# Three fused layers on one core: the scaling of the attention's exponentials on ScalarE, and v's rows laid out as long runs

## The chip, the cores and the metric

The kernel runs on one core of a Trainium2 chip. The metric is the device time of one execution in microseconds (us); lower is better. The engines are TensorE (PE), VectorE (DVE), ScalarE (ACT), GpSimd (POOL) and SyncE (SP), which issues the transfers here. Each works through its own list of instructions in order.

## What is computed

Local attention with block summaries, then a dense two-layer block, then a mixture of 8 experts with a capacity:

```python
scores_l = scale * np.matmul(q, k.transpose(0, 1, 3, 2))      # (2, 8, 768, 768), kept where |i - j| < 16
scores_s = scale * np.einsum('bhsd,bhnd->bhsn', q, k_sum) + np.log(block)   # 24 block summaries
a = np.exp(scores_all - np.max(scores_all, axis=-1, keepdims=True))
a = a / (np.sum(a, axis=-1, keepdims=True) + 1e-09)
x = np.matmul(a, np.concatenate([v, v_sum], axis=2))
h = x @ w_in
g = np.where(h > 0.0, h, np.exp(np.minimum(h, 0.0)) - 1.0)
x = g @ w_out                                                  # 1536 tokens, 512 -> 2048 -> 512
# then: every token goes to its best of 8 experts (relu MLP 512 -> 1024 -> 512), scaled by its gate
```

All of it is in float32. Matmuls of the dense layers split each operand into a high and a low part and add three products.

## The kernel before

Attention runs on 16 items `p`, a pair of heads for half a batch entry each, and each item in two **slots** `u` (32 in all) of three query blocks of 64. A block of 64 queries sees 96 keys around it and 24 block summaries, 120 columns. In a slot (names of the code):

- `pe_s` (L225): PE computes the scores S for three blocks.
- `dve_max` (L236): DVE adds the mask and takes the extreme; `act_exp` (L249): ACT takes three exponentials of 128x120 with their sums.
- `norm` (L256): DVE adds 1e-9 to the sums (L258) and takes the reciprocal (L259); POOL multiplies all three blocks by it in one operation of 128x360 (L260).
- `pe_t`, `act_t` (L263, L269): one slot later PE transposes the result, and ACT copies it from PSUM as pT (L271), at the start of the slot after that.
- `pe_o`, `act_o`, `dve_o`: PE multiplies pT by the tile `vw` (L279); ACT takes the high part of the result into xT (L288), DVE the low part (L293).

`vw` holds, for six query blocks, the 96 rows of v that each uses, and under them the 24 summaries. `load_vw` (L169) brings the 96 rows by one transfer on SP's queue from the padded v, whose rows are 512 values of all heads; 128 of them belong to a pair. `load_vs` (L217) brings the summaries from SBUF. `prep_k` and `prep_va` make the keys' windows and the summaries for the next item, in the first and the second slot of each item.

The dense layer starts in slot 8 while the attention still runs. `w_load`, `w_conv` and `w_split` bring a block of weights as float64 words, make float32 of them in three steps on DVE (L315, L319, L322), and split it: ACT casts the high part (L328), POOL subtracts it (L329). `mm1` (L340) is the first matmul into a PSUM tile h, of which there are two; `elu_exp` (two on ACT, L346 and L347), `elu_max` (DVE, L351), `g_hi` (ACT, L356) and `g_lo` (POOL, L360) make g; `mm2` (L373) is the second matmul.

The whole is written out in one order by hand (`manual_schedule`), in the loop over `sl` from L830 on. Slots 0 to 7 are attention and weight conversion (the head). Slots 9 to 16 are the `dense` ones, with a block of the first and of the second weights converted in most of them; the first matmul runs two blocks ahead in them, so that slots 15 and 16 have none. From slot 17 on the order is the same for each slot, with one weight block converted and put away in DRAM per slot. In the dense slots `norm` stands between the second and third step of the conversion.

Of the kernel before, what the change touches and what calls it, by code (L numbers as in the profile page):

```python
# [15 lines left out]
ALU = mybir.AluOpType  # L16
# [4 lines left out]
P = 128  # L21
NB, NH, S, D = 2, 8, 768, 64
NPAIR = NH // 2
WIN = 16
BLK = 32
NSUM = S // BLK
QB = 64
NQB = S // QB
WK = QB + 2 * WIN
KEYS = WK + NSUM  # L30
N = NB * S
DM = NH * D
# [5 lines left out]
TT = 384  # L38
NT = N // TT
BPT = TT // P  # L40
QPT = TT // QB
# [5 lines left out]
GRP = 3  # L47


def build(tc, cap, qT, kT, vT, vP, wi, wo, wg, wgT, wx, out):  # L50
    nc = tc.nc
    cap = max(0, min(int(cap), N))
    nj = -(-cap // P)
# [3 lines left out]
    with ctx:  # L57
# [26 lines left out]
        for hh in range(2):  # L84
# [3 lines left out]
                out=mv, in_=mv, pattern=[[0, 3], [1, WK]], compare_op=ALU.is_ge,  # L88
                fill=NEG, base=-1, channel_multiplier=-1)
            nc.gpsimd.affine_select(  # L90
                out=mv, in_=mv, pattern=[[0, 3], [-1, WK]], compare_op=ALU.is_ge,
# [8 lines left out]
            out=tri, in_=tri, pattern=[[1, P]], compare_op=ALU.is_gt,  # L100
# [68 lines left out]
        def load_vw(p):  # L169
            t, pr = divmod(p, NPAIR)  # L170
            b, half = divmod(t, 2)
            vw = apool.tile([P, QPT, P], F32, tag="vw", name=f"vw{p}")
            vbase = (b * (S + 2 * WIN) + half * TT) * DM + pr * P
            nc.sync.dma_start(
                vw[0:WK], bass.AP(vP.tensor, vbase, [[DM, WK], [QB * DM, QPT], [1, P]]))
            VW[p] = vw

        def prep_k(p):
# [18 lines left out]
        def prep_va(p):  # L197
            t, pr = divmod(p, NPAIR)
            if t % 2 == 0:
                nc.vector.tensor_reduce(  # L200
                    out=VA[p % 2][:, WK:KEYS], in_=VT[p].rearrange("p (u s) -> p u s", s=BLK),
                    op=ALU.add, axis=AX.X)
# [18 lines left out]
        def where(u):  # L221
            p, g = divmod(u, GPP)
            return p, p // NPAIR, p % NPAIR, g * GRP
# [32 lines left out]
        def norm(u):  # L256
            sc, st = SC[u], ST.pop(u)
            nc.vector.tensor_scalar(out=st[:, 2], in0=st[:, 1], scalar1=1e-9, scalar2=None, op0=ALU.add)  # L258
            nc.vector.reciprocal(out=st[:, 2], in_=st[:, 2])  # L259
            nc.gpsimd.tensor_tensor(  # L260
                sc, sc, st[:, 2].unsqueeze(2).to_broadcast([P, GRP, KEYS]), op=ALU.mult)

        def pe_t(u):  # L263
            pt = PT[u] = psm(f"T{u}", "T")
# [25 lines left out]
        def dve_o(u):  # L290
            p, t, pr, g0 = where(u)
            q = slice(g0 * QB, (g0 + GRP) * QB)
            nc.vector.tensor_tensor(  # L293
                xT[t][:, 1, pr, q], PS.pop(("o", u))[:, 0 : GRP * QB], xT[t][:, 0, pr, q].bitcast(F32),
                op=ALU.subtract)
# [10 lines left out]
        def w_conv(which, parts=(0, 1, 2)):  # L306
            for part in parts:
                for io, f in which:
                    if part == 0:
                        raw = RW[io, f]  # L310
                        t = mpool.tile([P, 512], U32, tag="t1", bufs=T1, name=f"t1{io}{f}")
                        RW[io, f] = (raw[:, :, 0], raw[:, :, 1], t)
                    lo, hi, t = RW[io, f]
                    if part == 0:
                        nc.vector.tensor_scalar(  # L315
                            out=t, in0=hi, scalar1=3, scalar2=0x3FFFFFF8,
                            op0=ALU.logical_shift_left, op1=ALU.bitwise_and)
                    elif part == 1:
                        nc.vector.scalar_tensor_tensor(  # L319
                            out=t, in0=hi, scalar=0xC0000000, in1=t, op0=ALU.bitwise_and, op1=ALU.bitwise_or)  # L320
                    else:
                        nc.vector.scalar_tensor_tensor(  # L322
                            out=t, in0=lo, scalar=29, in1=t, op0=ALU.logical_shift_right, op1=ALU.bitwise_or)
# [30 lines left out]
        def g_hi(t, f):  # L354
            gT[t, f] = mpool.tile([P, 2, TT], F32R, tag="g", name=f"g{t}_{f}")
            nc.scalar.copy(gT[t, f][:, 0], EP[t, f])  # L356

        def g_lo(t, f, eng):
            g = gT[t, f]
            eng.tensor_tensor(g[:, 1], EP.pop((t, f)), g[:, 0].bitcast(F32), op=ALU.subtract)  # L360
# [359 lines left out]
        st = {}  # L720
# [50 lines left out]
        load_k(1)  # L771
        load_q(1)
        load_vw(0)
        prep_k(0)
        prep_va(0)
        pe_va(0)
        load_vt(1)
        load_vw(1)


# [29 lines left out]
        def w_prefetch():  # L810
            if nload[0] >= len(order) or (order[nload[0]] in later and len(put) < len(later)):
                return
            io, f = order[nload[0]]
            nload[0] += 1
            if (io, f) in later:
                t = mpool.tile([P, 512], U32, tag="raw", bufs=4, name=f"rw{io}{f}")
                nc.sync.dma_start(t, wf[later.index((io, f))])
                RW[io, f] = (None, None, t)
            else:
                w_load(io, f)  # L820
# [9 lines left out]
        for sl in range(total):  # L830
            n = sl - LAG
            u, p = sl, sl // GPP
# [25 lines left out]
            def split_next():  # L858
                if wpend:
                    w_split(*wpend.pop(0))  # L860

            if sl == LAG - 1:
# [30 lines left out]
                act_exp(u)  # L893
                prep_k(p + 1)
                norm(u)
                g_hi(0, 0)
                g_lo(0, 0, nc.gpsimd)
# [22 lines left out]
            if u < NU and sl % GPP == 1 and p and p + 1 < NPR:  # L920
                load_vw(p + 1)
# [21 lines left out]
            if dense:  # L943
                if el:
                    g_hi(*el[1:])
                    g_lo(*el[1:], nc.gpsimd)
                split_next()
                split_next()
                if sl % GPP and p + 1 < NPR:
                    prep_va(p + 1)  # L950
                w_conv(cv, (0,))
                if u - 2 in late:
                    dve_o(u - 2)
                w_conv(cv, (1,))
                norm(u)
                w_conv(cv, (2,))
                for x in cv:
                    w_prefetch()
                wpend.extend(cv)
                cv = []  # L960
# [16 lines left out]
            if u < NU and not dense:  # L977
                norm(u)
# [80 lines left out]
            if gr == 1 and t == 0 and f == FPG:  # L1059
                pa.close()  # L1060
                qpool = ctx.enter_context(tc.tile_pool(name="qpool", bufs=2, side="right"))
                pr = ExitStack()
# [71 lines left out]
        for f in range(4, 8):  # L1134
# [4 lines left out]
            out=key, in0=sel0, scalar=float(32 * N * NE), in1=key, op0=ALU.mult, op1=ALU.add)  # L1139
# [3 lines left out]
            op=ALU.is_gt)  # L1143
# [6 lines left out]
            op=ALU.is_equal)  # L1150
# [27 lines left out]
        for v in range(3):  # L1178
            nc.vector.tensor_reduce(
                out=tabs[:, :, v].rearrange("p (k j) -> p k j", j=nj), in_=tmp[v], op=ALU.add, axis=AX.X)  # L1180
# [109 lines left out]
        large(1, cv1)  # L1290


_NAMES = ["qT", "kT", "vT", "vP", "wi", "wo", "wg", "wgT", "wx"]


def _layout(np, q, k, v, moe_w_in, moe_w_out, moe2_w_gate, moe2_w1, moe2_w2):
    c = np.ascontiguousarray
    qT = q.reshape(NB, NPAIR, 2, S, D).transpose(0, 1, 2, 4, 3).reshape(NB, NPAIR, P, S)
    kT = k.reshape(NB, NPAIR, 2, S, D).transpose(0, 1, 2, 4, 3).reshape(NB, NPAIR, P, S)
    kT = np.pad(kT, ((0, 0), (0, 0), (0, 0), (WIN, WIN)))  # L1300
    vT = v.reshape(NB, NPAIR, 2, S, D).transpose(0, 1, 2, 4, 3).reshape(NB, NPAIR, P, S)
    vP = np.pad(v.transpose(0, 2, 1, 3).reshape(NB, S, DM), ((0, 0), (WIN, WIN), (0, 0)))
    wi = moe_w_in.reshape(NCC, P, NFC, P).transpose(2, 1, 0, 3).reshape(NFC, P, 512)
    wo = moe_w_out.reshape(NFC, P, DM)
    wi, wo = c(wi).view(np.int64), c(wo).view(np.int64)
    wg = moe2_w_gate.reshape(NCC, P, NE).transpose(1, 0, 2)
    w1 = moe2_w1.reshape(NE, NCC, P, 2, 512).transpose(0, 2, 3, 1, 4).reshape(NE, P, 8, 512)
    w2 = moe2_w2.reshape(NE, 8, P, DM).transpose(0, 2, 1, 3)
    wx = np.concatenate([w1, w2], axis=2)
    return {"qT": c(qT), "kT": c(kT), "vT": c(vT), "vP": c(vP), "wi": c(wi), "wo": c(wo), "wg": c(wg), "wgT": c(moe2_w_gate.T), "wx": c(wx)}  # L1310


# [16 lines left out]
```

## Time and profile before

| | before |
|---|---|
| runs shown | 517.78, 516.6, 513.6 us (median 516.6) |
| the profiled execution | 517.51 us, of which the profile's span is 515.6 |
| PE busy | 481.3 us (93%) |
| DVE busy | 335.3 us (65%) |
| ACT busy | 270.3 us (52%) |
| POOL busy | 196.5 us (38%), of it the scaling L260 31.4 us in 32 operations |
| transfers | 79.98 MB, of it 16 loads vw of 288 KB |

Times within the profile count from the span's start. A row of the timeline gives the start of an instruction (or of several equal ones), how long it took from its start to its end, waiting for a resource included, its engine, line, operation, the tiles it writes and reads, and in brackets how long the engine stood idle before it and who released it.

### The profile page before, as it was taken

Reading aid. Unit: us, or ns where it says so; the run is one execution under the profiler, and the core shown is the slowest. Engines: PE = TensorE matmul, PEld = TensorE weight load, DVE = VectorE, ACT = ScalarE, POOL = GpSimd, SP = SyncE. Lnnn points to the kernel's source line nnn. Section 1 sums busy time; section 2 is a strip of 40 time slices with the busy share of each in tenths; the row PEclk is TensorE's granted clock in tenths of the full one; section 3 lists DMA queues with packets and bytes.
Section 4 is the critical chain, followed back from the end, with each engine's and each line's share of the span. In section 5 each row is a group of like instructions: output and inputs, shape, how many; then the busy total and the mean of one; then the engine's idle time right before and its main releaser. Section 6 shows DMA issues by size and latency. Waiting matters only on the chain. (4 is left out here: it accounts for less than half of the span.)

```text
span 515.6 us, 9263 instructions
## 1 busy us (share of the span) xinstructions
PE 481.3 (93%) x3052; PEld 414.0 (80%) x3052; DVE 335.3 (65%) x887; ACT 270.3 (52%) x688; POOL 196.5 (38%) x197
## 2 busy tenths in 40 slices
PE   6888798899999999999999999999998999999792
PEld 5576576688888888999999999888867989888682
DVE  3689999899888772111128979856686864556460
ACT  3846555675657546665333333333753865566350
POOL 4345575635333443785223323322335030040440
PEclk8988998999999999999999999999999999999897
DMA  8996555678776432438310010011644976357470
GB/s 219 258 266 200 168 177 188 207 231 257 210 192 185 160 103 66 112 112 285 123 52 11 0 62 0 2 62 57 211 142 144 334 220 225 124 182 252 147 244 15
DMA packets 45635, 79.98 MB, mean 155 GB/s; under 512 B 4604, under 2 KB 19196, under 8 KB 45552
## 3 DMA queue, kind: packets, MB, share of 16 engines
q1 hardware_dynamic: 43792, 73.83, 46.5%
q0 software_dynamic: 1760, 5.19, 3.3%
q8 instruction: 34, 0.56, 0.5%
q14 instruction: 49, 0.40, 0.3%
HBM read 65.29 MB, written 13.11 MB: 152 GB/s over the span
## 5 line engine op out<-in xcount | busy, mean ns | idle before, releaser
L340 PE MATMUL h<-xT,Wi 128*128 128x384 f32 x768 | 150.4, 344 | 8.3 <-DVE e L351 6.6
L340 PEld LDWEIGHTS h<-xT,Wi 128*128 128x128 f32 x768 | 138.2, 192 | 15.9 <-DVE e L351 8.8
L373 PE MATMUL acc<-Wo,g 128*128 128x512 f32 x576 | 146.8, 398 | 1.7 <-POOL Wo L329 1.0
L360 POOL TENSOR_TENSOR g<-e,g 128x384 fp32r<-128x384 f32 x63 | 77.2, 1226 | 124.2 <-ACT g L356 109.5
L373 PEld LDWEIGHTS acc<-Wo,g 128*128 128x128 f32 x576 | 105.3, 188 | 23.7 <-POOL g L360 1.4
L351 DVE SCALAR_TENSOR_TENSOR e<-e,h 128x384 f32<-128x384 f32 x64 | 35.3, 552 | 75.6 <-ACT e L347 75.6
L346 ACT ACTIVATE e<-h 128x384 f32<-128x384 f32 x64 | 31.6, 493 | 58.7 <-PE h L340 56.6
L260 POOL TENSOR_TENSOR sc<-sc,st 128x360 f32<-128x360 f32 x32 | 31.4, 980 | 68.6 <-DVE st L259 50.1
L565 DVE TENSOR_TENSOR E<-rawq,E 128x512 fp32r<-128x512 f32 x70 | 47.7, 722 | 10.9 <-ACT E L555 9.9
L252 ACT ACTIVATE sc<-sc,st 128x120 f32<-128x120 f32 x96 | 36.8, 385 | 28.7 <-DVE st L245 28.7
L356 ACT CAST g<-e 128x384 fp32r<-128x384 f32 x64 | 33.0, 516 | 33.0 <-DVE e L351 33.0
L697 PE MATMUL bh<-xbq,E 128*128 128x256 f32 (+1 forms) x288 | 43.6, 303 | 2.5 <-ACT ysf L601 1.4
L555 ACT CAST E<-rawq 128x512 fp32r<-128x512 f32 x75 | 42.5, 618 | 6.3 <-issue 3.2
L697 PEld LDWEIGHTS bh<-xbq,E 128*128 128x128 f32 x288 | 41.3, 188 | 4.8 <-ACT ysf L601 1.6
L686 PE MATMUL y<-E,g 128*128 128x512 f32 x168 | 41.7, 393 | 0.0
L435 DVE CUSTOM_DVE_ANT_0 dot<-a,wgb 128x512 f32<-128x512 f32 x48 | 40.0, 889 | 0.0
L686 PEld LDWEIGHTS y<-E,g 128*128 128x128 f32 x168 | 30.6, 188 | 5.7
L347 ACT ACTIVATE e<-e 128x384 f32<-128x384 f32 x64 | 33.7, 526 | 2.0
L271 ACT COPY pT<-T 120x384 f32<-120x384 f32 x32 | 15.3, 479 | 36.7 <-PE T L267 36.4
L245 DVE CUSTOM_DVE_ANT_0 sc<-S,masks 128x120 f32<-128x120 f32 x96 | 22.0, 277 | 11.1 <-PE S L231 10.3
L231 PE MATMUL S<-kw,qt 64*64 64x120 f32 x384 | 28.9, 287 | 0.0
L231 PEld LDWEIGHTS S<-kw,qt 64*64 64x64 f32 x384 | 21.3, 143 | 6.1 <-issue 3.9
(216 smaller groups left out, 621.5 us busy)
## 6 DMA issues: line engine op xcount, KB each, us to landing
rawq<-wx SPq DMA_DIRECT2D x88, 256.0 KB
rawi<-wi SPq DMA_DIRECT2D x16, 512.0 KB
rawo<-wo SPq DMA_DIRECT2D x16, 512.0 KB
vw<-vP SPq DMA_DIRECT2D x16, 288.0 KB
kt<-kT SPq DMA_DIRECT2D x8, 400.0 KB
qt<-qT SPq DMA_DIRECT2D x16, 192.0 KB
vt<-vT SPq DMA_DIRECT2D x8, 384.0 KB
out<-xg SPq DMA_DIRECT2D x12, 256.0 KB
```

Of the source, the lines that this page charges most:

```text
L231: nc.tensor.matmul(ps[r, gi * KEYS : (gi + 1) * KEYS], lhsT=QT[p][r, (g0 + gi) * QB : (g0 + gi + 1) * QB], rhs=KW[p][r, g0 + gi, :], start ...
L252: nc.scalar.activation(out=sc[:, gi], in_=sc[:, gi], func=AF.Exp, bias=st[:, 0, gi : gi + 1], scale=-1.0, accum_out=st[:, 1, gi : gi + 1])
L340: nc.tensor.matmul(HP[t, f][:, 0:TT], lhsT=w[:, s, c * P : (c + 1) * P], rhs=xT[t][:, xs, c, :], start=c == 0 and n == 0, stop=c == NCC - ...
L347: nc.scalar.activation(out=e, in_=e, func=AF.Relu, bias=1.0, scale=-1.0)
L351: nc.vector.scalar_tensor_tensor(out=e, in0=e, scalar=-1.0, in1=h[:, 0:TT], op0=ALU.mult, op1=ALU.max)
L360: eng.tensor_tensor(g[:, 1], EP.pop((t, f)), g[:, 0].bitcast(F32), op=ALU.subtract)
L373: nc.tensor.matmul(accp[tb], lhsT=g[:, s, tb * P : (tb + 1) * P], rhs=w[:, ws], start=f % FPG == 0 and n == 0, stop=f % FPG == FPG - 1 and ...
L435: nc.vector.tensor_tensor_reduce(out=junk, in0=x2[t * BPT + tb], in1=WGB[e // 2][:, e % 2], scale=1.0, scalar=0.0, op0=ALU.mult, op1=ALU.a ...
L555: (nc.vector.tensor_copy if m in vec else nc.scalar.copy)(EW[k][m][:, 0], raw_of(k, m))
L565: (nc.gpsimd if m in pool else nc.vector).tensor_tensor(w[:, 1], raw, w[:, 0].bitcast(F32), op=ALU.subtract)
L686: nc.tensor.matmul(ys[b], lhsT=g[:, s, b * P : (b + 1) * P], rhs=w[:, ws], start=f == 0 and n == 0, stop=f == 7 and n == 2)
L697: nc.tensor.matmul(h[:, 0:nt], lhsT=EW[k][half * NCC + c][:, ws, fc * P : (fc + 1) * P], rhs=xb[:, s, c, 0:nt], start=n == 0, stop=n == 3 ...
```

## The change

The 96 rows of v that each query block uses are laid out ahead of the launch as one array `vW`, in which a row of the tile (one key position, six blocks, 128 values) is one run of 3,072 bytes. The load reads these runs. The multiplication by the reciprocal becomes three operations on ACT, one for each block, with the reciprocal as a scale per partition. In the dense slots `norm` moves ahead of the second conversion step.

```diff
-            vbase = (b * (S + 2 * WIN) + half * TT) * DM + pr * P
-            nc.sync.dma_start(
-                vw[0:WK], bass.AP(vP.tensor, vbase, [[DM, WK], [QB * DM, QPT], [1, P]]))
+            nc.sync.dma_start(vw[0:WK], vW[b, half, pr])
...
-            nc.gpsimd.tensor_tensor(
-                sc, sc, st[:, 2].unsqueeze(2).to_broadcast([P, GRP, KEYS]), op=ALU.mult)
+            for gi in range(GRP):
+                nc.scalar.mul(out=sc[:, gi], in_=sc[:, gi], mul=st[:, 2, gi : gi + 1])
...
                 if u - 2 in late:
                     dve_o(u - 2)
+                norm(u)
                 w_conv(cv, (1,))
-                norm(u)
                 w_conv(cv, (2,))
...
+    vW = np.stack([vP[:, i * QB : i * QB + WK] for i in range(NQB)], axis=1)
+    vW = vW.reshape(NB, 2, QPT, WK, NPAIR, P).transpose(0, 1, 4, 3, 2, 5)
```

Behind the load, the lines of the changed kernel have numbers lower by two (L258 and L259 are L256 and L257 there, L322 is L320); the new operations on ACT are its L259. In the rows that follow, `sc` is the tile of exponentials, `st` the sums and reciprocals.

ACT in the head, slots 2 and 3, before:

```order
L213 ACTIVATE vs_271<-V_250 24x128
L252 ACTIVATE sc_276,st_277<-sc_276,st_277 128x120 x3
L288 CAST xT_284<-O_264 128x192
L191 COPY kw_286<-kt_192 128x6x64
L271 COPY pT_315<-T_301 120x384
L252 ACTIVATE sc_328,st_329<-sc_328,st_329 128x120 x3
L288 CAST xT_284<-O_317 128x192
L271 COPY pT_365<-T_349 120x384
```

and of the change:

```order
L211 ACTIVATE vs_275<-V_254 24x128
L250 ACTIVATE sc_280,st_281<-sc_280,st_281 128x120 x3
L286 CAST xT_288<-O_268 128x192
L189 COPY kw_290<-kt_192 128x6x64
L259 ACTIVATE sc_280<-sc_280,st_281 128x120 x3
L269 COPY pT_321<-T_307 120x384
L250 ACTIVATE sc_334,st_335<-sc_334,st_335 128x120 x3
L286 CAST xT_288<-O_323 128x192
L259 ACTIVATE sc_334<-sc_334,st_335 128x120 x3
L269 COPY pT_373<-T_357 120x384
```

The three operations L259 of a slot now stand ahead of pT of the slot before it, which opens the next slot.

DVE in a dense slot (slot 10: t1o and t1i are the two weight blocks under conversion), before:

```order
L315 TENSOR_SCALAR t1o_776<-rawo_627 128x512
L315 TENSOR_SCALAR t1i_778<-rawi_653 128x512
L293 TENSOR_TENSOR xT_765<-O_743,xT_765 128x192
L319 SCALAR_TENSOR_TENSOR t1o_776<-rawo_627,t1o_776 128x512
L319 SCALAR_TENSOR_TENSOR t1i_778<-rawi_653,t1i_778 128x512
L258 TENSOR_SCALAR st_757<-st_757 128x3
L259 RECIPROCAL st_757<-st_757 128x3
L322 SCALAR_TENSOR_TENSOR t1o_776<-rawo_627,t1o_776 128x512
L322 SCALAR_TENSOR_TENSOR t1i_778<-rawi_653,t1i_778 128x512
```

and of the change:

```order
L313 TENSOR_SCALAR t1o_796<-rawo_643 128x512
L313 TENSOR_SCALAR t1i_798<-rawi_669 128x512
L291 TENSOR_TENSOR xT_785<-O_763,xT_785 128x192
L256 TENSOR_SCALAR st_777<-st_777 128x3
L257 RECIPROCAL st_777<-st_777 128x3
L317 SCALAR_TENSOR_TENSOR t1o_796<-rawo_643,t1o_796 128x512
L317 SCALAR_TENSOR_TENSOR t1i_798<-rawi_669,t1i_798 128x512
L320 SCALAR_TENSOR_TENSOR t1o_796<-rawo_643,t1o_796 128x512
L320 SCALAR_TENSOR_TENSOR t1i_798<-rawi_669,t1i_798 128x512
```

The two operations on the sums stand two conversion operations earlier.

ACT where the dense slots end (the end of slot 16, slot 17), before:

```order
L356 CAST g_7_1256<-e_7_1243 128x384
L191 COPY kw_1263<-kt_1093 128x6x64
L271 COPY pT_1291<-T_1280 120x384
L252 ACTIVATE sc_1304,st_1305<-sc_1304,st_1305 128x120 x3
L288 CAST xT_765<-O_1293 128x192
L382 COPY a_0_1329<-acc_0_0_796 128x512
```

and of the change:

```order
L354 CAST g_7_1288<-e_7_1275 128x384
L259 ACTIVATE sc_1278<-sc_1278,st_1279 128x120 x3
L189 COPY kw_1297<-kt_1121 128x6x64
L269 COPY pT_1325<-T_1314 120x384
L250 ACTIVATE sc_1338,st_1339<-sc_1338,st_1339 128x120 x3
L286 CAST xT_785<-O_1327 128x192
L259 ACTIVATE sc_1338<-sc_1338,st_1339 128x120 x3
L380 COPY a_0_1365<-acc_0_0_818 128x512
```

In each slot three operations have come in on ACT. From slot 18 on they stand ahead of the cast that makes the high part of g.

## Rows read from the trace of the kernel before

**Rows 1.** Busy us of each engine by stage: PE, PEld, DVE, ACT, POOL, clock, DMA share, GB/s.

```profile
10.00:25.00 15.00, 13.76 (x151) 9.71 (x149) 11.07 (x54) 12.33 (x51) 5.46 (x10) 0.93 0.95 257
...
46.00:94.00 48.00, 40.01 (x289) 32.66 (x286) 47.32 (x101) 27.56 (x86) 31.54 (x24) 0.93 0.59 179
...
117.00:188.00 71.00, 71.00 (x574) 61.42 (x575) 59.99 (x173) 42.24 (x142) 30.24 (x25) 1.00 0.62 184
188.00:515.60 327.60, 311.79 (x1683) 273.31 (x1682) 176.58 (x446) 159.34 (x319) 106.22 (x94) 0.99 0.40 128
```

**Rows 2.** Timeline of ACT in slots 2 to 4: start, length, line, tiles.

```profile
15.51 0.40 ACT L252 ACTIVATE sc<-sc,st 128x120 f32<-128x120 f32 x1 [0.81 <-DVE st L245]
...
17.00 0.52 ACT L191 COPY kw<-kt 128x384 f32<-128x384 f32 x1
17.42 0.48 ACT L271 COPY pT<-T 120x384 f32<-120x384 f32 x1
...
19.20 0.30 ACT L288 CAST xT<-O 128x192 fp32r<-128x192 f32 x1
19.44 0.48 ACT L271 COPY pT<-T 120x384 f32<-120x384 f32 x1
...
20.91 0.40 ACT L252 ACTIVATE sc<-sc,st 128x120 f32<-128x120 f32 x1 [0.70 <-DVE st L245]
```

**Rows 3.** Timeline of DVE in the head, with the idle time before.

```profile
17.61 0.18 DVE L259 RECIPROCAL st<-st 128x3 f32<-128x3 f32 x1
...
26.27 0.95 DVE L200 TENSOR_REDUCE va<-vt 128x24 f32<-128x768 f32 x1 [2.16 <-DMA vt<-vT]
```

**Rows 4.** Timeline of POOL: the scaling in the head and in a dense slot.

```profile
17.96 0.79 POOL L260 TENSOR_TENSOR sc<-sc,st 128x360 f32<-128x360 f32 x1 [0.84 <-ACT pT L271]
...
68.04 1.24 POOL L260 TENSOR_TENSOR sc<-sc,st 128x360 f32<-128x360 f32 x1
```

**Rows 5.** Timeline of DVE in a dense slot.

```profile
63.62 0.69 DVE L319 SCALAR_TENSOR_TENSOR t1o<-rawo,t1o 128x512 uint32<-128x512 uint32 x1
64.22 1.50 DVE L319 SCALAR_TENSOR_TENSOR t1i<-rawi,t1i 128x512 uint32<-128x512 uint32 x1
65.64 1.24 DVE L258 TENSOR_SCALAR st<-st 128x3 f32<-128x3 f32 x1
...
67.01 1.62 DVE L322 SCALAR_TENSOR_TENSOR t1o<-rawo,t1o 128x512 uint32<-128x512 uint32 x1
68.55 1.27 DVE L322 SCALAR_TENSOR_TENSOR t1i<-rawi,t1i 128x512 uint32<-128x512 uint32 x1
```

**Rows 6.** Timeline of ACT: the first copy of slot 17, the last cast of slot 18.

```profile
100.17 0.47 ACT L271 COPY pT<-T 120x384 f32<-120x384 f32 x1
...
109.51 0.51 ACT L356 CAST g<-e 128x384 fp32r<-128x384 f32 x1
```

**Rows 7.** Timeline of PE in slots 17 and 19.

```profile
100.70 0.57 PE L279 MATMUL O<-pT,vw 120*64 120x64 f32 x12
...
112.59 1.85 PE L373 MATMUL acc<-Wo,g 128*128 128x512 f32 x7 [0.72 <-POOL g L360]
```

**Rows 8.** Timeline of ACT, 117 to 188 us: the idle time before pT.

```profile
122.98 0.48 ACT L271 COPY pT<-T 120x384 f32<-120x384 f32 x1 [1.97 <-PE T L267]
...
158.87 0.48 ACT L271 COPY pT<-T 120x384 f32<-120x384 f32 x1 [0.91 <-PE T L267]
```

**Rows 9.** ACT's groups by line, 100 to 190 us: busy us, mean ns of one.

```profile
L252 ACT ACTIVATE sc<-sc,st 128x120 f32<-128x120 f32 x45 | 17.2, 384 | 3.4 <-DVE st L245 3.4
...
L213 ACT ACTIVATE vs<-V 24x128 f32<-24x128 f32 x3 | 0.8, 270 | 0.1
```

**Rows 10.** SP's queue, 92.6 to 94.2 and 237 to 250 us: packets, MB, share.

```profile
q1 hardware_dynamic: 669, 0.39, 77.7%
...
q1 hardware_dynamic: 1687, 4.11, 92.6%
```

**Rows 11.** Waits over the whole span: us in total, times, longest.

```profile
PEld O L279 <- ACT pT L271: 4.5, 20, 0.7
```

More of the change, by code (lines that the diff above doesn't have):

```diff
@@ L47, with build @@
 GRP = 3
-def build(tc, cap, qT, kT, vT, vP, wi, wo, wg, wgT, wx, out):
+def build(tc, cap, qT, kT, vT, vW, wi, wo, wg, wgT, wx, out):
     nc = tc.nc
@@ L1290, in build @@
         large(1, cv1)
-_NAMES = ["qT", "kT", "vT", "vP", "wi", "wo", "wg", "wgT", "wx"]
+_NAMES = ["qT", "kT", "vT", "vW", "wi", "wo", "wg", "wgT", "wx"]
 def _layout(np, q, k, v, moe_w_in, moe_w_out, moe2_w_gate, moe2_w1, moe2_w2):
@@ L1309, in _layout @@
     wx = np.concatenate([w1, w2], axis=2)
-    return {"qT": c(qT), "kT": c(kT), "vT": c(vT), "vP": c(vP), "wi": c(wi), "wo": c(wo), "wg": c(wg), "wgT": c(moe2_w_gate.T), "wx": c(wx)}
+    return {"qT": c(qT), "kT": c(kT), "vT": c(vT), "vW": c(vW), "wi": c(wi), "wo": c(wo), "wg": c(wg), "wgT": c(moe2_w_gate.T), "wx": c(wx)}
 def kernel(q, k, v, moe_w_in, moe_w_out, moe2_w_gate, moe2_w1, moe2_w2, moe2_capacity):
```

## The prediction

> **What bounds the kernel now.** I read the busy times stage by stage first [rows 1]. From 117 to 188 us TensorE (PE) is busy for all 71.00 of 71.00 us, and from 188 on for 312 of 328. What the change can move therefore lies before 117. From 46 to 94 VectorE (DVE) is busy 47.32 of 48.00 us and PE only 40.01: DVE is the bound, and PE waits for its products. From 10 to 25 no engine is full: ScalarE (ACT) has 12.33 of 15.00, the DMA engines 0.95 of their time. There the slots are a chain over engines. One slot is scores on PE, masked minimum on DVE, three exponentials on ACT, sums and reciprocal on DVE, scaling on GpSimd (POOL), transposes on PE, a copy on ACT.
>
> Then I read the timelines. In the head two slots (one pair of heads) take 5.40 us, from the exponentials at 15.51 to those at 20.91 [rows 2]. The reciprocal ends at 17.79 and POOL scales from 17.96 for 0.79 us [rows 3, 4]. ACT does not wait for it: it copies pT at 17.42. In slot 5 the head stands 2.16 us for the transfer of vt [rows 3].
>
> In the DVE-bound stage the reader is to see five DVE rows between 63.62 and 69.75 [rows 5]. The first passes in 0.69. The others, the same kind of work on the same size, take 1.50, 1.62 and 1.27, and a scaling of 3 columns takes 1.24. Each began while a POOL operation was running and ended with it or just after it: DVE and POOL take turns. POOL's scaling at 68.04 lasts 1.24 there against 0.79 at 17.96 [rows 4]. So POOL's work costs DVE time, and the change takes one of POOL's four operations out of the slot.
>
> **The change, part by part.** *The layout of v.* Sixteen loads of 288 KB come as 96 runs of 3,072 bytes and no longer as 576 of 512. Alone on the queue such a load ran in the 1.6 us around 93 us, with 669 packets, 0.39 MB at 77.7% of the engines' time, so 314 GB/s of busy time; a stretch of long runs (237 to 250 us) moved 4.11 MB at 92.6%, 341 GB/s [rows 10]. A load so gets about 8% cheaper, 0.1 us of some 1 us, and in the worst reading of these rows 0.3. Nobody waits for vw: what O, which reads it, waits for is ACT's copy of pT, 4.5 us in 20 waits [rows 11]. I take 0, covered by that copy; at most it shortens the one vt stall, 2.16.
>
> *The scaling moves to ACT.* 32 POOL operations go, 96 ACT operations of 128x120 come. No such row exists. Nearest is the same ACTIVATE without a sum over 128 columns: 270 ns [rows 9]; three are 0.81 us a slot, which I take. Below stands the cast of 192 columns, whose successor starts 0.24 later (19.20 to 19.44) [rows 2]: 0.7. Above stands the exponential of the same shape, which also reads out a sum: 384 ns [rows 9], 1.15.
>
> [...]
>
> *The wait that comes with it.* ACT runs in order. The three copies stand behind the next k-block's copy and before pT of the following slot, and wait for DVE's reciprocal. pT, then O on PE, then the next exponentials queue behind them. In the head: from the exponentials (15.51) to the reciprocal's end (17.79) are 2.28; then 0.81, then pT 0.48: 3.6 a slot, 7.2 a pair, and 0.27 for vs once a pair: 7.4 against 5.40, so +2.0 a pair. Slot 2's exponentials come about 0.95 late (the first copies push vs, exponentials and pT), slot 4's 2.95, slot 5's 3.95. Of that the vt stall covers 2.16, since vt is there by the time: +1.8 in slot 6. Two POOL scalings that collided with DVE's weight conversion in slots 5 to 8 are gone; half a turn of 0.6 is my estimate, 0.3. **Head: +1.5.**
>
> *The norm ahead of the second conversion step, DVE-bound stage.* The norm now stands before POOL's first operation has begun, costs about 0.3 unblocked, and the ACT copies fall in ACT's idle time (27.56 of 48 busy [rows 1]). POOL keeps three operations, and each still blocks one DVE operation: 0.3, then 1.50 (behind g), about 1.8 (behind Wo: the 1.24 less 0.1 and its own 0.6), 1.62 (behind Wi), and 0.6 free: 5.9 instead of 6.13 [rows 5]. That is 0.2 a slot over six slots, **-1.2**. What bounds it: nothing, if the turns end as late as now; at most the whole last block, 1.27 less 0.69, 0.6 a slot, -3.5.
>
> *Slots 14 to 18, 86 to 117 us, where PE takes over as bound.* Slots 15 and 16 have no first matmul and are short, and ACT works there without a gap until pT at 100.17, right behind which O starts on PE at 100.70 [rows 6, 7]. Two groups of copies go in front of it: 1.6 later, and 0.3 more from slot 14, whose copies push pT too. In slot 18 g (109.51) [rows 6] moves behind the copies and pT behind g: O comes about 1.0 later, but the stall of 0.72 of the second matmul, which waits for POOL's g behind POOL's scaling, goes [rows 7]. **+2.2.**
>
> *117 to 188 us.* ACT stands idle 1.97 us or more before pT in each slot but one, and 0.91 there, where the three copies of acc precede it [rows 8]; the new copies take 0.81 and wait some 0.1 for the reciprocal, so they just fit there and fit easily elsewhere. g reaches POOL about 0.9 later, but POOL no longer scales for 1.06 before it. **0.** Without that idle time each of 12 slots would lose about 0.9.
>
> **Sum.** 517.51 us (the profiled execution, span 515.6) + 1.5 - 1.2 + 2.2 = 520.0. The median of the runs shown, 516.6, lies 0.9 below that execution: 519.1.
>
> **Rivals.** *Scaling as dear as the exponentials* (slower). With 1.15 a slot instead of 0.81, seven head slots add 2.4 and three at the takeover 1.0, and if DVE's turns save nothing, 1.2: 4.6 on my sum, 523.7. For it: the same shape, the same operand per partition. Against: the exponentials also read out a sum.
>
> *DVE gets back the whole of POOL's scaling* (faster). If the whole of its 1.24 leaves each of the six slots from 46 to 94, 7.4 go and not 1.2; with head and takeover as above (3.7) that is -3.7, on the median's scale 512.9. Beyond -1% it comes only where the copies also hide in the head (+1.5 becomes 0 or less): 511.4. For it: DVE is full there and PE waits for it. Against: of 1.27 in the last row only 0.6 is blocked, and the norm ahead of the first turn just lets g block another operation. [...]
>
> *The head is bound by transfers after all* (no change). If the cheaper vw loads bring vt 2.16 earlier and the copies hide in the idle time that ACT has in the head, the head gives -2.2 and not +1.5: 515.4.
>
> That the new layout of v moves nothing is my own case.
>
> **How the numbers follow.** About 1%, 5 us, is what a measurement of this kernel can tell from no change. My case, 516 to 522, has 0.53; the transfer-bound head 0.13; the dear scaling 0.22, all of it counted beyond +1%; the relief of DVE 0.12, two thirds of it beyond -1%, where the head gives back too. So faster 0.08, same 0.70, slower 0.22. The range reaches from the relief of DVE (512.9), and so past the cheap copies with the last block gone (0.7 a slot takes 1.1 off the ten slots, DVE 2.3 more: 515.7) and the transfer-bound head (515.4), to the dear scaling (523.7): 513 to 524.
>
> **What would show it.** In the changed profile: the pair in the head takes about 7.4 us, the ACT copies begin right at the reciprocal's end, ACT is the fullest engine from 10 to 25 us; three blocked DVE operations a slot from 46 to 94, with slots of 8.0 us; at about 102 PE stands for pT before O; from 117 on PE is full as before. I am wrong if the copies start with ACT still waiting for something else, if slots between 46 and 94 fall below 7.5 us, or if PE stalls between 117 and 188.

## The result, and the profile after

The changed kernel takes 521.72 us in the median (520.62 to 523.15, 4 runs) against 516.62 us. The ratio is 1.0107, 95% interval 1.0073 to 1.0141, so about 1% slower. The forecast was 519.1 us, within 513 to 524: inside the range, but the change is +5.1 us for a forecast +2.5. The profiled execution took 520.65 us, its span is 518.7.

Busy us by stage, columns as in [rows 1], with the stretch from 94 to 117 us added:

```profile
10.00:25.00 15.00, 12.01 (x126) 8.51 (x121) 8.50 (x40) 13.02 (x51) 1.66 (x5) 0.89 0.77 243
...
46.00:94.00 48.00, 39.50 (x300) 32.21 (x301) 45.47 (x110) 35.52 (x118) 24.51 (x17) 0.96 0.58 181
94.00:117.00 23.00, 19.73 (x172) 16.39 (x171) 16.05 (x60) 19.77 (x66) 4.59 (x4) 1.00 0.72 227
117.00:188.00 71.00, 71.00 (x575) 61.23 (x574) 46.55 (x171) 52.71 (x178) 16.16 (x12) 1.00 0.59 185
188.00:518.70 330.70, 311.55 (x1691) 273.56 (x1689) 176.60 (x447) 160.10 (x321) 107.75 (x94) 0.99 0.39 127
```

ACT is now the fullest engine from 10 to 25 us (13.02 of 15.00), and has 8 us more from 46 to 94. PE is full from 117 to 188 as before. The last line is the surprise: PE is as busy in it as before (311.55 us against 311.79 [rows 1]), but the stretch is 330.70 and not 327.60 long. No instruction of it was changed.

The new operation in the page's list of groups (L259; of the lines below it, the numbers are 2 lower than before):

```profile
L259 ACT ACTIVATE sc<-sc,st 128x120 f32<-128x120 f32 x96 | 30.9, 385 | 8.3 <-DVE st L257 8.1
```

One lasts 385 ns, and ACT stands idle 8.1 us in all because its copies wait for the reciprocal. In the timeline of ACT in the head, the rows that answer to [rows 2]:

```profile
15.76 0.40 ACT L250 ACTIVATE sc<-sc,st 128x120 f32<-128x120 f32 x1
...
18.13 0.96 ACT L259 ACTIVATE sc<-sc,st 128x120 f32<-128x120 f32 x3 [0.36 <-DVE st L257]
19.00 0.46 ACT L269 COPY pT<-T 120x384 f32<-120x384 f32 x1
...
21.62 0.96 ACT L259 ACTIVATE sc<-sc,st 128x120 f32<-128x120 f32 x3 [0.77 <-DVE st L257]
22.49 0.45 ACT L269 COPY pT<-T 120x384 f32<-120x384 f32 x1
...
23.27 0.40 ACT L250 ACTIVATE sc<-sc,st 128x120 f32<-128x120 f32 x1
```

The pair of slots takes 23.27 - 15.76 = 7.51 us instead of 5.40. ACT waits for the reciprocal, scales, and only then copies pT. Three copies end 0.96 after they start, but the next instruction starts 0.87 after them (18.13 to 19.00): overlapping neighbours, they occupy 0.87.

The timeline of DVE in the same dense slot as [rows 5], from the norm (L256) on:

```profile
64.07 0.16 DVE L256 TENSOR_SCALAR st<-st 128x3 f32<-128x3 f32 x1
...
64.35 1.52 DVE L317 SCALAR_TENSOR_TENSOR t1o<-rawo,t1o 128x512 uint32<-128x512 uint32 x1
65.80 1.76 DVE L317 SCALAR_TENSOR_TENSOR t1i<-rawi,t1i 128x512 uint32<-128x512 uint32 x1
67.48 1.78 DVE L320 SCALAR_TENSOR_TENSOR t1o<-rawo,t1o 128x512 uint32<-128x512 uint32 x1
69.18 0.68 DVE L320 SCALAR_TENSOR_TENSOR t1i<-rawi,t1i 128x512 uint32<-128x512 uint32 x1
```

The norm is free (0.16, for 1.24 [rows 5]), three conversion steps stretch while POOL's three operations run (from 64.31 to 68.71), the last passes in 0.68.

PE at the takeover, to be set against [rows 7]:

```profile
96.39 0.57 PE L277 MATMUL O<-pT,vw 120*64 120x64 f32 x12 [0.83 <-ACT pT L269]
...
101.61 0.57 PE L277 MATMUL O<-pT,vw 120*64 120x64 f32 x12 [1.29 <-ACT pT L269]
...
112.77 0.57 PE L277 MATMUL O<-pT,vw 120*64 120x64 f32 x12 [1.14 <-ACT pT L269]
```

PE, the bound there, stands for pT three times; the stall of 0.72 for POOL's g is gone.

After 188 us the place that costs most is at about 453 us, where PE's list jumps over an arm of the expert code that was not taken. PE's timeline there, first of before, then of the changed kernel:

```profile
448.73 4.24 PE L686 MATMUL y<-E,g 128*128 128x512 f32 x18
453.33 4.58 PE L697 MATMUL bh<-xbq,E 128*128 128x256 f32 x36 [0.36 <-issue]
```

```profile
449.78 4.24 PE L684 MATMUL y<-E,g 128*128 128x512 f32 x18
457.41 4.58 PE L695 MATMUL bh<-xbq,E 128*128 128x256 f32 x36 [3.39 <-issue]
```

PE idles 3.39 us ahead of `bh` where it idled 0.36, and waits for nothing that the profile shows.

A second place hides part of that loss. Behind a later jump both executions pause for 2 us, and the same 18 matmuls follow, before and changed:

```profile
479.16 6.00 PE L623 MATMUL bh<-E,xbq 128*128 128x512 f32 x18 [2.02 <-issue]
```

```profile
483.15 4.44 PE L621 MATMUL bh<-E,xbq 128*128 128x512 f32 x18 [1.93 <-issue]
```

The granted clock of the 6 us from their start was 0.72 before and 1.00 in the changed kernel, and the stretch up to the matmuls `bt` (at 491.55 and 493.39) is 2.2 us longer before. So the two lengths do not differ by the gap alone. The changed kernel is 1.1 us late ahead of the gap, loses 3.0 in it, gains 2.2 here, and loses some 1.2 more up to the end.

### The profile page after: what moved, and what is told of

Read it like the earlier page. It is cut to its first block, busy times and chain, and to the rows that moved or that the text cites. A ratio compares the mean times of both kernels' runs of the same rounds, so it can differ in the third digit from the quotient of the medians.

```text
span 518.7 us, 9266 instructions
## 1 busy us (share of the span) xinstructions
PE 476.4 (92%) x3052; PEld 410.3 (79%) x3052; DVE 313.7 (60%) x887; ACT 298.7 (58%) x784; POOL 164.9 (32%) x165
## 5 line engine op out<-in xcount | busy, mean ns | idle before, releaser
L338 PE MATMUL h<-xT,Wi 128*128 128x384 f32 x768 | 147.2, 339 | 5.3 <-DVE e L349 4.9
L338 PEld LDWEIGHTS h<-xT,Wi 128*128 128x128 f32 x768 | 136.0, 189 | 12.6 <-DVE e L349 6.6
L358 POOL TENSOR_TENSOR g<-e,g 128x384 fp32r<-128x384 f32 x63 | 74.0, 1174 | 203.5 <-ACT g L354 187.2
L371 PEld LDWEIGHTS acc<-Wo,g 128*128 128x128 f32 x576 | 106.4, 189 | 22.8 <-POOL Wo L327 1.1
L563 DVE TENSOR_TENSOR E<-rawq,E 128x512 fp32r<-128x512 f32 x70 | 46.5, 706 | 8.0 <-ACT E L553 6.8
L250 ACT ACTIVATE sc<-sc,st 128x120 f32<-128x120 f32 x96 | 36.7, 383 | 16.7 <-DVE st L243 16.6
L243 DVE CUSTOM_DVE_ANT_0 sc<-S,masks 128x120 f32<-128x120 f32 x96 | 21.8, 276 | 23.9 <-PE S L229 23.9
L259 ACT ACTIVATE sc<-sc,st 128x120 f32<-128x120 f32 x96 | 30.9, 385 | 8.3 <-DVE st L257 8.1
L277 PE MATMUL O<-pT,vw 120*64 120x64 f32 x384 | 18.5, 233 | 12.6 <-ACT pT L269 10.9
L277 PEld LDWEIGHTS O<-pT,vw 120*64 120x64 f32 x384 | 14.1, 139 | 19.0 <-ACT pT L269 17.4
```

Of the source, the lines that this page charges most:

```text
L250: nc.scalar.activation(out=sc[:, gi], in_=sc[:, gi], func=AF.Exp, bias=st[:, 0, gi : gi + 1], scale=-1.0, accum_out=st[:, 1, gi : gi + 1])
L277: nc.tensor.matmul(po[hh * D : (hh + 1) * D, gi * QB : (gi + 1) * QB], lhsT=VW[p][0:KEYS, g0 + gi, hh * D : (hh + 1) * D], rhs=pT[0:KEYS, ...
L338: nc.tensor.matmul(HP[t, f][:, 0:TT], lhsT=w[:, s, c * P : (c + 1) * P], rhs=xT[t][:, xs, c, :], start=c == 0 and n == 0, stop=c == NCC - ...
L371: nc.tensor.matmul(accp[tb], lhsT=g[:, s, tb * P : (tb + 1) * P], rhs=w[:, ws], start=f % FPG == 0 and n == 0, stop=f % FPG == FPG - 1 and ...
L563: (nc.gpsimd if m in pool else nc.vector).tensor_tensor(w[:, 1], raw, w[:, 0].bitcast(F32), op=ALU.subtract)
```

## The experiments

One execution's start wanders (the masked minimum of slot 2, DVE's L243 or L245, starts between 13.4 and 15.8 us), so I compare stretches between the starts of a slot's first masked minimum in DVE's timeline. "Gap" is PE's idle time ahead of that `bh`, "jump" the length of the branch before it on PE's own sequencer, in the trace's raw records. A ratio stands to the runs of before made beside it on the same chip.

| kernel | slots 2-8 | 8-14 | 14-31 | gap | jump | median | ratio, 95% interval |
|---|---|---|---|---|---|---|---|
| before | 28.96 | 42.19 | 97.27 | 0.36 | 0.95 | 516.62 | |
| after | 31.61 | 40.09 | 99.27 | 3.39 | 3.48 | 521.72 | 1.0107, 1.0073 to 1.0141 |
| layout | 28.24 | 42.01 | 97.25 | none | 0.39 | 514.74 | 0.9988, 0.9959 to 1.0016 |
| order_only | 29.55 | 42.35 | 97.42 | 0.58 | 1.48 | 516.04 | 1.0005, 0.9974 to 1.0035 |
| scale_only | 30.42 | 40.48 | 99.10 | 3.05 | 3.42 | 521.84 | 1.0103, 1.0058 to 1.0147 |
| scale_and_order | 31.38 | 40.05 | 99.28 | 3.45 | 3.80 | 523.62 | 1.0129, 1.0089 to 1.0169 |
| after_pad | 31.57 | 40.05 | 99.26 | 0.34 | 1.31 | 518.51 | 1.0069, 1.0042 to 1.0097 |
| before_cut | 28.04 | 41.92 | 97.27 | 3.25 | 3.42 | 521.67 | 1.0121, 1.0084 to 1.0158 |
| steady_only | 29.38 | 42.17 | 97.15 | 0.34 | 1.32 | 515.54 | 0.9993, 0.9969 to 1.0017 |
| dense_only | 27.87 | 39.43 | 97.42 | none | 1.03 | 513.30 | 0.9949, 0.9922 to 0.9977 |
| head_only | 31.59 | 41.60 | 97.24 | none | 0.39 | 518.71 | 1.0071, 1.0041 to 1.0100 |
| takeover_only | 26.94 | 41.99 | 99.22 | 0.84 | 1.51 | 516.38 | 1.0035, 1.0007 to 1.0063 |
| late | 29.17 | 39.88 | 97.25 | none | 0.32 | 514.13 | 0.9993, 0.9964 to 1.0022 |
| late_from9 | 29.17 | 40.23 | 97.26 | none | 0.33 | 512.47 | 0.9952, 0.9922 to 0.9982 |

### The parts alone

*layout*: the changed kernel with scaling and order of before.

> Only the layout of v is changed; scaling and order are as before. Theory 1 (the loads of vw are waited for by nobody): the head, the dense slots and the start of the full stretch stand as before, scores of slot 20 at 116.9 +- 0.3 us, the vt stall of slot 5 stays (2.16, shorter by at most 0.3), time ratio 0.997 to 1.003. Theory 2 (the 2 to 4 us that the changed kernel loses after 188 us come from the layout): the front as before, but the time 2 to 4 us above before, ratio 1.004 to 1.008, with wider gaps on TensorE after 188. Theory 3 (cheaper loads bring vt earlier): the stall of 2.16 goes, the maximum of slot 8 comes up to 2.2 earlier, ratio 0.996.

The ratio's interval includes 1. No long jump, no gap, all stretches as before: the layout is worth nothing that these runs can tell, and the loss after 188 us isn't its. The stall for vt, in the DVE timelines of this kernel, of takeover_only (same layout) and of the changed one:

```profile
24.78 0.95 DVE L198 TENSOR_REDUCE va<-vt 128x24 f32<-128x768 f32 x1 [1.87 <-DMA vt<-vT]
```

```profile
24.97 0.95 DVE L198 TENSOR_REDUCE va<-vt 128x24 f32<-128x768 f32 x1 [0.57 <-DMA vt<-vT]
```

```profile
26.03 0.95 DVE L198 TENSOR_REDUCE va<-vt 128x24 f32<-128x768 f32 x1
```

It is anything from 0.57 to 2.61 (order_only) from one execution to the next, and none, or 0.21 at most, in the five kernels in which ACT scales ahead of pT in the head.

*scale_and_order*: the changed kernel with the old load of v.

> Scaling on ScalarE and the norm moved, but v in its old layout. Theory 1 (the layout moves nothing): the front is that of the changed kernel, pair in the head 7.5 us, maximum of slot 8 at 45.4, slots of 7.85 between 46 and 94, scores of slot 20 at 118.2; and the time is the changed kernel's, 1.003 to 1.011 of before. Theory 2 (the loss after 188 us comes from the layout): the same front, but a time only 1.3 us above before, ratio 1.001 to 1.004.

The front is the changed kernel's, and so are the gap and the whole loss. It comes with the scaling. Its 1.0129 lies above the 1.003 to 1.011 of theory 1, though its interval does not; the clock behind the gap, below, added to it in the profiled execution.

*order_only* and *scale_only*: before with

```diff
+                norm(u)
                 w_conv(cv, (1,))
-                norm(u)
```

and before with the three copies of L259 in place of POOL's operation.

> The norm stands ahead of the second conversion step, but GpSimd scales as before. Theory 1 (what shortens the dense slots is that GpSimd's fourth operation leaves): the norm itself is free (0.3 instead of 1.4 us), but four conversions are blocked and not three, some 1.5, 1.7, 1.7 and 1.2: slots of 8.2 to 8.4 us as before, scores of slot 20 at 116.9 to 117.5, ratio 0.999 to 1.003. Theory 2 (the order is what saves): slots of 7.8, scores of slot 20 at 114 to 115, ratio 0.995.

> ScalarE scales, but the norm stays behind the second conversion step and v in its old layout. Theory 1 (GpSimd's operation leaving is the whole gain): three blocked operations again, one of them the norm's sum (1.24); slots of 7.7 to 7.9, head as in the changed kernel (pair 7.5), scores of slot 20 at 118.2 +- 0.5. Theory 2 (the order is needed): the copies begin 2.8 us later in the slot than in the changed kernel, the transposes, pT and O follow, and the slots stay at 8.2 to 8.4; scores of slot 20 at 120 or later, 3 us above before.

DVE in a dense slot of order_only has a free norm and four blocked steps:

```profile
63.59 1.52 DVE L319 SCALAR_TENSOR_TENSOR t1o<-rawo,t1o 128x512 uint32<-128x512 uint32 x1
65.03 1.75 DVE L319 SCALAR_TENSOR_TENSOR t1i<-rawi,t1i 128x512 uint32<-128x512 uint32 x1
66.71 1.78 DVE L322 SCALAR_TENSOR_TENSOR t1o<-rawo,t1o 128x512 uint32<-128x512 uint32 x1
68.41 1.27 DVE L322 SCALAR_TENSOR_TENSOR t1i<-rawi,t1i 128x512 uint32<-128x512 uint32 x1
```

So the order alone gives nothing, as theory 1 had it. The scaling alone gives 1.7 of the 2.1 us from slot 8 to 14, but half of it before slot 10; in the four slots from 10 to 14 it takes 32.37 us, against 33.16 before and 31.36 with both. There the copies start later in the slot, and DVE waits for what ACT does behind them, 0.18 us in this slot of the 0.25 that a slot is longer:

```profile
63.77 0.55 DVE L351 SCALAR_TENSOR_TENSOR e<-e,h 128x384 f32<-128x384 f32 x1 [0.18 <-ACT e L347]
```

Theory 1 said 7.7 to 7.9 a slot, theory 2 8.2 to 8.4; it is 8.1. As I read it, the order serves to let the copies begin early.

### The gap at 453 us

The changed kernel, scale_only and scale_and_order have it; before, layout and order_only, which scale on POOL, don't. What the three share on PE: its list holds 16 waits fewer (92 against 108), all ahead of 188 us, so that everything later stands 16 places earlier. Two kernels change only that.

after_pad, against the changed kernel:

```diff
-        busy(24)
+        busy(32)
```

before_cut, against before:

```diff
-        busy(24)
+        busy(16)
```

> The changed kernel with 8 more warm-up transposes on TensorE at the very start (32 and not 24), while it waits for the first loads: TensorE's program has then as many instructions ahead of each later one as before's, since the change took 16 waits out of it and a transpose is two instructions. Theory 1 (the jump of TensorE's sequencer at about 450 us costs 3.5 us and not 0.4 to 1.5 because the code stands 16 instructions earlier): the jump is short again, the gap of 3.4 us ahead of bh at 457 falls to 0.6 or less, time about 3 us below the changed kernel, 518.5, ratio to before 1.002 to 1.006. Theory 2 (the gap comes from what ScalarE or the other engines do): the gap stays at 3.0 to 3.5, ratio 1.010 to 1.013.

> The kernel before with 8 warm-up transposes fewer (16 and not 24), so that TensorE's code stands 16 instructions earlier, as in the changed kernel; nothing else. Theory 1 (position of the code): a gap of 3.0 to 3.5 us ahead of bh at about 453 appears, time 2.5 to 3 us above before, ratio 1.005 to 1.007. Theory 2 (the gap comes from ScalarE's or other engines' work): the tail as before, ratio 0.998 to 1.002.

PE ahead of `bh`, in after_pad and in before_cut:

```profile
454.32 4.58 PE L695 MATMUL bh<-xbq,E 128*128 128x256 f32 x36 [0.34 <-issue]
```

```profile
455.19 6.99 PE L697 MATMUL bh<-xbq,E 128*128 128x256 f32 x36 [3.25 <-issue]
```

The gap goes in the one and comes in the other, without any change to scaling or layout. The position of PE's code decides it. The times agree less sharply. before_cut's 1.0121 lies above the 1.005 to 1.007 of its theory 1. after_pad's 1.0069 lies a little above its 1.002 to 1.006, and 0.4% or 2 us below the changed kernel's 1.0107, a step that the two intervals alone would not tell from none. Over all fourteen kernels, PE's code stood 16 places earlier than before's in the four with a jump of 3.4 to 3.8 us; in the ten others it stood 5 or 3 earlier, the same, or 10 to 25 later, and the jump took 0.3 to 1.5. A second branch, right behind the next load of a count, takes 2.4 to 3.5 in all fourteen. In the kernel before, the jump of 0.95 and a second one of 2.98 end at 453.28, 0.31 behind the 18 matmuls in the rows above (4.24 us, to 452.97), so PE hides nearly all of both; in the changed kernel the two take 3.48 and 3.46 and end at 457.35, 3.33 behind the same matmuls.

The trace also shows what a long jump goes with. Two queues bring instructions, and all that q8 brings are blocks of 16,384 bytes. Its line in the view of the transfers, first of before from 446.5 to 448.7 us, ahead of its jump at 448.75, then of the changed kernel from 449.8 to 453.3, within its jump at 449.81:

```profile
q8 instruction: 1, 0.02, 2.6%
```

```profile
q8 instruction: 1, 0.02, 1.6%
```

The changed kernel has no such block from 430 to 449.8 us. In the ten kernels with a short jump the block starts 0.9 to 5.1 us ahead of the jump, in the four with a long one 0.7 to 1.5 us after the jump has begun. In all ten kernels in which the jump takes longer than 0.4 us, it ends 2.3 to 2.7 us after the block's start. So a jump is short where the block was already on its way, and the second branch, whose block never starts ahead of it, is long everywhere. That q8 serves PE is read from this agreement; no view names the engine.

Why 16 places turn the order of block and jump round, no run shows. The order flips between 5 and 16 places; none of the runs moved the code in smaller steps, so the place where it does isn't shown either.

before_cut loses more than its gap. Its 36 matmuls take 6.99 us after it, not 4.58. The granted clock of the 7 us behind the gap, in the windows of the changed kernel's profiled execution and of scale_and_order's:

```profile
457.40:464.40 7.00, 6.99 (x52) 6.73 (x53) 4.06 (x8) 5.11 (x12) 1.81 (x2) 1.00 0.47 135
```

```profile
457.60:464.60 7.00, 7.00 (x37) 7.00 (x38) 2.29 (x5) 3.31 (x8) 1.69 (x2) 0.60 0.42 116
```

After a pause of 3.4 us the granted clock was 1.00 in the one execution and 0.60 in the other; it was 0.61 in before_cut and 0.79 in scale_only. Where it is lower, up to 2.5 us are lost on top (7.07 against 4.58 for the 36 matmuls in scale_and_order).

### Each stretch alone

The edit of all four kernels is a condition on the slot, here dense_only's; the others have POOL and ACT in other slots, and put `norm(u)` back behind the second conversion step. head_only also has 28 warm-up transposes.

```diff
-            for gi in range(GRP):
-                nc.scalar.mul(out=sc[:, gi], in_=sc[:, gi], mul=st[:, 2, gi : gi + 1])
+            if LAG <= u < 14:
+                for gi in range(GRP):
+                    nc.scalar.mul(out=sc[:, gi], in_=sc[:, gi], mul=st[:, 2, gi : gi + 1])
+            else:
+                nc.gpsimd.tensor_tensor(
+                    sc, sc, st[:, 2].unsqueeze(2).to_broadcast([P, GRP, KEYS]), op=ALU.mult)
```

`LAG` is 9.

> ScalarE scales only in the 13 slots from 19 on, GpSimd in the others; norm at its old place, v in its new layout, TensorE's code as long as before's. Theory 1 (from 117 on the copies fit into ScalarE's idle time): TensorE full from 117 to 188, the time from slot 20 to slot 31 as before within 0.3, no gap at 453, ratio 0.997 to 1.002. Theory 2 (the copies push pT and O, 0.9 a slot): 5 to 11 us lost between slots 20 and 31, ratio 1.010 to 1.02.

> ScalarE scales only in slots 9 to 13, GpSimd in the others; the norm moved and v in its new layout as in the changed kernel. TensorE's code stands 5 instructions earlier than before's. Theory 1 (the head and the takeover are what the copies cost, the VectorE-bound slots what they give): the head as before, 0.45 us less in each of the five slots, nothing lost from slot 14 on: scores of slot 20 about 2.2 us earlier than before, no gap at 453, ratio 0.993 to 0.998. Theory 2 (what the five slots give is lost at the takeover in any case, since TensorE's work is due there): scores of slot 20 within 0.7 us of before, ratio 0.998 to 1.001.

> ScalarE scales only in slots 0 to 8, GpSimd in the others; norm at its old place, v in its new layout; 4 more warm-up transposes keep TensorE's code at before's place. Theory 1 (the head loses what the copies and the late pT cost there, and nothing gives it back): from the maximum of slot 2 to that of slot 8 some 31.2 us as in the changed kernel, against 28.7 on average in the kernels that scale on GpSimd there; all later stretches as before; ratio 1.003 to 1.007. Theory 2 (the transfer of vt covers most of it, as forecast): 29.5 to 30.2, ratio 1.000 to 1.003.

> ScalarE scales only in slots 14 to 18, GpSimd in the others; norm at its old place, v in its new layout. Theory 1 (pT and so O stand behind the copies while TensorE takes over as the bound): 2.0 us more than before between the maxima of slots 14 and 31 (99.3 against 97.3), all else as before, ratio 1.002 to 1.006. Theory 2 (the loss there in the changed kernel is only the gain of the VectorE-bound slots given back, since TensorE's work is due): 97.3 as before, ratio 0.997 to 1.001.

All four went by theory 1, head_only a little above its numbers (31.59 for 31.2, 1.0071 for 1.007 at most). From 19 on the copies cost nothing that can be measured (slots 14 to 31 in 97.15; from slot 20 alone 0.4 more, not within the 0.3 that I gave it, but slot 20 came earlier by as much). Slots 9 to 13 give 2.6 us with nothing lost behind. The head costs 31.59 against 28.5, the mean of the eight kernels that leave the head's order alone or nearly (before, layout, order_only, before_cut, steady_only, dense_only, takeover_only, late_from9), which spread from 26.94 to 29.55; its time is up by 3.7 us (2.1 to 5.2). The takeover costs 99.22 against 97.3, 1.8 us of time (0.4 to 3.2). Together 3.7 + 1.8 - 2.6 = 2.9, near the 3.6 of after_pad, which is the change without the gap.

### Is it the work or the order?

In late, `norm(u)` only notes the slot in a list, and `act_scale` makes the copies one slot later; against the changed kernel:

```diff
-            for gi in range(GRP):
-                nc.scalar.mul(out=sc[:, gi], in_=sc[:, gi], mul=st[:, 2, gi : gi + 1])
+            LATE.append((sc, st))
...
                 act_t(u - 2)
                 if u != NU:
                     pe_o(u - 2)
+            act_scale()
```

The order of slot 8 is written out by itself and has the same call behind its pT; the list and `act_scale` are left out here. late_from9 is the same with POOL scaling in slots 0 to 8 and 24 warm-up transposes.

> The changed kernel with the three copies of a slot one slot later in ScalarE's order, behind the next pT and ahead of the next exponentials, so that pT no longer stands behind a wait for the reciprocal; 8 more warm-up transposes keep the long jump of TensorE short. Theory 1 (the order costs, not the work): head 29.5 to 30.3 from slot 2 to slot 8 (the exponentials still stand behind the copies), slots 8 to 14 in 40.1 as in the changed kernel, slots 14 to 31 in 97.3 to 97.6, ratio 0.996 to 1.002. Theory 2 (ScalarE's added 0.87 us a slot is the cost, wherever it stands): 31.4, 40.1 and 99.3 as in the changed kernel, ratio 1.005 to 1.009.

> GpSimd scales in slots 0 to 8, ScalarE from slot 9 on, with the copies behind the next pT; norm moved and v in its new layout. Theory 1 (as in the run before, without the head's loss): 28.7 from slot 2 to slot 8, 40.1 or less from 8 to 14, 97.3 to 97.6 from 14 to 31, ratio 0.993 to 0.998. Theory 2 (the added work is the cost): 99.3 from 14 to 31, ratio 0.998 to 1.002.

ACT of late in the head, and PE at the takeover, in slots 17 and 19:

```profile
15.04 0.39 ACT L250 ACTIVATE sc<-sc,st 128x120 f32<-128x120 f32 x1
...
19.68 0.47 ACT L276 COPY pT<-T 120x384 f32<-120x384 f32 x1
20.55 0.97 ACT L266 ACTIVATE sc<-sc,st 128x120 f32<-128x120 f32 x3 [0.40 <-DVE st L257]
...
21.84 0.39 ACT L250 ACTIVATE sc<-sc,st 128x120 f32<-128x120 f32 x1
```

```profile
97.38 0.57 PE L284 MATMUL O<-pT,vw 120*64 120x64 f32 x12 [0.85 <-ACT pT L276]
...
107.99 0.57 PE L284 MATMUL O<-pT,vw 120*64 120x64 f32 x12 [0.17 <-ACT pT L276]
```

pT goes ahead of the copies. PE still stands for it at the takeover, but for 0.85 and 0.17 us and not for 0.83, 1.29 and 1.14. The same copies now cost nothing from slot 14 to 31 (97.25 against 97.3): there it is what stands in front of pT, the wait and the copies behind it, that cost 2.0 us, not ACT's work.

In the head the work itself counts too. The pair still takes 6.80 us (15.04 to 21.84), between 5.40 and 7.51, since the copies now stand ahead of the exponentials. That slots 2 to 8 take 29.17, 0.7 above the mean of the heads left alone and within their spread, goes with a shorter wait for vt (0.84) and with slots 6 to 8, which take 14.60 for the changed kernel's 15.46.

late_from9 and dense_only, both half a per cent faster than before with intervals that exclude 1, beat both kernels.

## Why the prediction was near, step by step

The time lies in the forecast range, but the change was twice the forecast. That the sum of the front came out is partly luck, and the tail was left out of the forecast.

- **The layout of v, 0.** Right (layout). The stall of 2.16 that it might have shortened was a chance size of that one execution.
- **The price of the copies, 0.81 a slot.** Measured 0.87, so the rival that put them at the exponentials' 1.15 fell.
- **The head, +1.5.** The mechanism was right: pair 7.51 against 7.4, ACT fullest, the copies right behind the reciprocal. The term was mis-sized: 31.3, the mean of the five kernels with the changed head, less 28.5 is +2.8. From slot 2 to 6 the change costs 2.2 (15.8 less 13.6 in those means) where 1.8 were forecast. I had set the vt stall of one execution against it, 2.16; in the eight heads left alone it is 1.7 on average. No head with the copies ahead of pT was held up by transfers for more than 0.21, so the rival of the transfer-bound head fell. The larger part of the miss is in slots 6 to 8. There I had taken 0.3 off for collisions with the weight conversion that go, and they became 0.6 longer (15.5 against 14.9 in the means; the heads left alone spread from 14.53 to 15.75). late, with the same copies behind pT, takes 14.60 there: the delay of pT costs there too.
- **The VectorE-bound slots, -1.2.** Measured -2.1 (42.2 to 40.1). Three blocked steps a slot, as forecast, and slots of 7.8 us for the forecast 8.0. Mis-sized was the saving of a slot, 0.45 (slots 10 to 14) and not 0.2. Part of that is a slip: the five costs that the prediction lists add up to 5.8 and not 5.9, so 0.3 a slot and some -1.9. Of a POOL operation of 1.24 us DVE got back about a third, so the rival that gave it the whole fell.
- **The takeover, +2.2.** Measured +2.0, with the waits of O for pT at the places named.
- **117 to 188 us, 0.** Right: PE full, and steady_only the same as before.
- **The sum, +2.5.** The three measured terms give 2.8 - 2.1 + 2.0 = +2.7, and after_pad, the change without the gap, 3.6 (2.2 to 5.0). The sum was good by luck: the errors of the head (1.3 too little) and of the dense slots (0.9 too little saved) cancelled.
- **What the prediction lacked.** It took everything behind 188 us as unmoved, since no instruction there was changed. But 16 waits had gone from PE's list, a jump became 2.5 us longer, and PE lost 3.0 us there in the profiled execution, in others up to 2.5 more with the clock. That covers the 2.6 us by which the forecast was too low. How much of the 5.1 it is, the runs tell only roughly: 3.0 by the trace, 2 by the ratios of the changed kernel and after_pad.

## What to carry to other kernels

Moving an operation to an engine with idle time cost here what stood behind it in that engine's order (2.0 us from slot 14 to 31, and nothing with the same copies behind pT): look for a wait that lands ahead of a copy the bound engine needs, and put the moved work behind that copy. Where the chain runs through that engine anyway, as in the head here, the work cost wherever it stood (7.51 and 6.80 us a pair, for 5.40). Size a term from the stretch in which it acts, and over several executions where a transfer's arrival enters it. After a change, look at stretches with branches too: fewer instructions can shift all later code, and a jump that was hidden may no longer be (here 16 waits fewer, and 3.39 us of idle time for 0.36); padding PE's list tells that apart in one run.

## What the runs showed of the hardware

The jump at about 450 us on PE's sequencer took 0.3 to 1.5 us in ten kernels and 3.4 to 3.8 in the four whose code stood 16 places earlier. Wherever it took longer than 0.4, it ended 2.3 to 2.7 us after a block of 16,384 bytes had started on an instruction queue. The long one put 3.1 to 3.5 us of idle time on PE. After such a pause the same 36 matmuls took 4.58 to 7.07 us, at a granted clock of 1.00 to 0.60; after a pause of 2.0 us the same 18 matmuls took 4.44 us in one execution, at 1.00, and 6.00 in another, at 0.72. Eight warm-up transposes fewer at the start made the kernel 1.2% slower, as much as the whole change under study; in its profiled execution the gap (2.9 us more) and the slower clock behind it (2.4) make most of that.
